# Rational layer: the order of VectorE's subtraction after ScalarE's reads of the tile h

## The chip, the cores and the metric

The kernel runs on one core of a Trainium2 chip. The metric is the device time of one execution in microseconds (us); the time of a kernel is the median of its runs. A profiled execution also has a span: the time from its first to its last instruction.

## The reference, cut to what matters

Three layers run one after the other: a recurrent attention over 4 x 8 heads and 768 steps, a mixture of 8 experts on 3072 tokens of width 320, and a rational layer on the same tokens. Only the last is touched:

```python
def _moe2_ref(x, w_in, w_out, a, b):        # x [3072, 320], w_in [320, 2048], w_out [2048, 320]
    h = x @ w_in
    h2 = h * h
    h3 = h2 * h
    P = a[0] + a[1] * h + a[2] * h2 + a[3] * h3
    Q = 1.0 + np.abs(b[0]) * np.abs(h) + np.abs(b[1]) * h2
    g = P / (Q + 1e-06)
    return g @ w_out
```

## The kernel before, in words

Matrix products are done to nearly full fp32 precision with split operands: a value v becomes a rounded high part and the rest v - high (low part), and each product is the sum of high x high, low x high and high x low.

**Tiling of the rational layer.** The 3072 tokens are cut into 8 groups of 384. In each group the 2048 columns of `w_in` are cut into 8 pieces of 256. One piece of one group is a step m; there are 64 steps, numbered m = 8 G + mm, with mm from 0 to 7. A step's two halves of 128 columns land in two PSUM banks of the tile `h`, which has three banks of 128 x 512: the middle bank always holds the second half, and the first half alternates between the outer banks, bank 2 in even and bank 0 in odd steps (`outer`, L1150). So in every step one outer bank holds no part of the step's own product.

**The steps' order** is written out by hand (list `order`, L1318, run by `s3_step`, L1324), with the lag of each piece of work in steps. For each engine, in the order of its queue in step m:
- TensorE: `g_in(m)` (L1181): 8 matmuls into the outer bank (called A here), in some steps three transposes (below, called T), 8 matmuls into the middle bank (B); then `g_out(m-4)` (L1288): 18 matmuls into the output banks (O).
- ScalarE: `e_gh(m-3)` (L1277), then in some steps the copy of the transposed columns (L1077), then `e_p1(m)` (L1211, line 1214) and `e_abs(m)` (L1222), both reading h of both halves, `e_u(m)` for m < 7 only (L1230), and `e_y(m-1)` (L1255) and `e_s(m-1)` (L1261), which write the PSUM tile `s` (one buffer from step 3 on).
- VectorE: `e_t(m-2)` (L1265), `e_r(m-2)` (L1269), in some steps `e_prep(m)` (L1199), `e_g(m-2)` (L1273), then `e_p2(m)` (L1242) and `e_p3(m)` (L1247), which read h.
- GpSimd: `e_gl(m-3)` (L1284), `e_u(m)` from m = 7 on (L1232), `e_w(m)` (L1238), and in the steps mm = 4, 5 and 6 the scatter of one finished output tile (L129).

**Preparing the next group.** The 384 x 320 inputs of the next group have to be transposed into three pieces of columns (kk = 0, 1, 2) and split. This lies in the last three steps of a group, mm = 5, 6 and 7, of the groups 0 to 6: 21 steps, called prep steps here; the others are called plain. In a prep step `g_prep` (L1170) uses the free outer bank: TensorE transposes into it (L1101), ScalarE copies it into the high part `xh` (or `xr` for kk = 2; `xsplit`, part 0, L1077), and later, where `e_prep` stands in the order, VectorE subtracts the high part from it (`xsplit`, part 1, L1082) into the low part `xl` (for kk = 2 into the upper half of `xr`).

**What waits for what.** The framework orders readers of one PSUM tile on different engines after each other, and it takes `h` as one tile, whichever bank is meant. Where the kernel wants no order it says so: `other_bank` (L1165) declares that two instructions do not depend on each other, and `bank_free` (L1158) adds the wait that is needed. `sr["reads", m]` is the list of the instructions that have read h of step m so far: when `e_prep(m)` is called it holds `e_p1(m)` and `e_abs(m)`, both of ScalarE.

Of the kernel before, what the change touches and what calls it, by code (L numbers as in the profile page):

```python
# [8 lines left out]
F32 = mybir.dt.float32  # L9
# [5 lines left out]
ALU = mybir.AluOpType  # L15
# [6 lines left out]
def kernel(  # L22
# [17 lines left out]
    nc = tc.nc  # L40
# [100 lines left out]
    sx, sr = {}, {}  # L141
# [211 lines left out]
    with actx:  # L353
# [24 lines left out]
        for _ in range(12):  # L378
# [11 lines left out]
            out=bmask, in_=bmask, compare_op=ALU.is_ge, fill=0.0, base=0,  # L390
# [3 lines left out]
            out=bmask, in_=bmask, compare_op=ALU.is_ge, fill=0.0, base=D - 1,  # L394
# [512 lines left out]
        for g in range(3):  # L907
# [4 lines left out]
            out=grpf, in0=grpf, in1=cend.unsqueeze(1).broadcast_to([NH, B * 3, NCH]), op=ALU.mult  # L912
# [125 lines left out]
        out=mall, in0=macc.unsqueeze(1).broadcast_to([128, NE, JS, NE]),  # L1038
        in1=perm.unsqueeze(2).broadcast_to([128, NE, JS, NE]), op=ALU.mult,
# [30 lines left out]
    def xsplit(kk, pt, xs, part=None):  # L1070
        n = pt.shape[1]
        if part != 1:
            if kk < 2:
                xs += [xp.tile([128, 512], F32R, name=f"x{v}{kk}", bufs=2)[:, 0:n] for v in "hl"]
            else:
                xs.append(xp.tile([128, 512], F32R, name="xr", bufs=2)[:, 0:n])
            hi = nc.scalar.activation(out=xs[2 * kk], in_=pt, func=AF.Copy)  # L1077
            if part == 0:
                return hi.ins
        if part != 0:  # L1080
            xh, xl, r = (xs[2 * kk], xs[2 * kk + 1], slice(0, 128)) if kk < 2 else (xs[4], xs[4], slice(64, 128))
            nc.vector.tensor_tensor(out=xl[r], in0=pt[r], in1=xh[r].bitcast(F32), op=ALU.subtract)  # L1082

    wouth_d = dram.tile([DFF, DM], F32, name="wouth_d")
    woutl_d = dram.tile([DFF, DM], F32, name="woutl_d")
# [79 lines left out]
    def other_bank(products, reads):  # L1165
        for p in products:
            for r in reads:
                tc.declare_no_dep(p, r, reason="another bank")

    def g_prep(G, kk, m):  # L1170

        pt = sr["h"][:, outer(m + 1), 0:TG]
        bank_free(transposes(sx["xt4", NE + G], kk, pt), m - 1)
        sr["prep", m] = (kk, pt, sx["x", NE + G])
        sr["pcopy", m] = xsplit(*sr["prep", m], part=0)
        if kk == 2:
            ids = xp.tile([128, 4], I32, name="ids", bufs=3)
            nc.gpsimd.tensor_copy(ids[:, 0:NJ], sx["xt4", NE + G][:, 0:NJ, XI - 1].bitcast(I32))
            sx["ids", NE + G] = ids
# [18 lines left out]

    def e_prep(m):  # L1199
        if ("prep", m) in sr:  # L1200
            xsplit(*sr["prep", m], part=1)

    def tl(pool, name, tag, bufs, dt=F32):
        return pool.tile([128, 2, TG], dt, name=name, tag=tag, bufs=bufs)
# [104 lines left out]
    def e_store(m, j):  # L1309
# [8 lines left out]
    order = [  # L1318
        (3, e_gh), (3, e_gl), (LAG + 1, e_osb), (0, g_in), (0, e_p1), (0, e_abs), (0, e_u), (0, e_w), (LAG, g_out),
        (2, e_t), (2, e_r), (0, e_prep), (2, e_g), (1, e_y), (1, e_s), (0, e_p2), (0, e_p3),  # L1320
        *((LAG + 1 + j, e_store, j) for j in range(NJ)),
    ]
# [10 lines left out]
    with ExitStack() as mctx:  # L1333
# [95 lines left out]
        def x_prep(e, kk, pt=None):  # L1429
            n = width(e) if e < NE else TG  # L1430
            if pt is None:
                pt = ps_t.tile([128, 512], F32, name="pt")[:, 0:n]
            transposes(sx["xt4", e], kk, pt)
            xsplit(kk, pt, sx["x", e])
            if kk == 2:
                j = (n + 127) // 128
                if e < NE:
                    g0 = e * JS + slots(e)[0]
                    nc.gpsimd.tensor_copy(head[:, g0:g0 + j, :], sx["xt4", e][:, 0:j, 0:XI])
                else:  # L1440
                    ids = xp.tile([128, 4], I32, name="ids", bufs=3)
                    nc.gpsimd.tensor_copy(ids[:, 0:j], sx["xt4", e][:, 0:j, XI - 1].bitcast(I32))
                    sx["ids", e] = ids
# [99 lines left out]
        with tc.tile_pool(name="ov", bufs=1) as ov, tc.tile_pool(name="ovp", bufs=1, space=PSUM) as ovp:  # L1543
            total = nc.values_load(cnt_i[:, NE:NE + 1], min_val=0, max_val=NT)
            with tc.If(total > 0):
# [20 lines left out]
                for e in range(NE):  # L1566
                    n_e = nc.values_load(nt_i[:, e:e + 1], min_val=0, max_val=NTILE)
                    with tc.If(n_e > 0):
# [3 lines left out]
                            out=mk, in0=ekey, scalar1=float(NE - e), scalar2=-(2.0**20), op0=ALU.is_equal, op1=ALU.mult  # L1572
# [6 lines left out]
                        for t in range(NTILE):  # L1579
                            nc.gpsimd.indirect_dma_start(  # L1580
                                out=over[:, :], out_offset=bass.IndirectOffsetOnAxis(ap=idx[:, t:t + 1], axis=0),
# [5 lines left out]
                            out=mk, in0=tokf, scalar1=past[:, e:e + 1], scalar2=2.0**20, op0=ALU.is_ge, op1=ALU.mult  # L1587
# [6 lines left out]
                        with tc.For_i(0, n_e, 1) as t:  # L1594
# [3 lines left out]
                                out=xo, out_offset=None, in_=x_rows[:, :],  # L1598
# [21 lines left out]
                            for _ in gates(ov, go, xo[:, 0:XI].unsqueeze(1), "o"):  # L1620
# [3 lines left out]
                                out=yo[:, 1:], in0=py, scalar1=go, scalar2=None, op0=ALU.mult  # L1624
                            )
                            nc.gpsimd.indirect_dma_start(
                                out=y_sorted[:, :], out_offset=bass.IndirectOffsetOnAxis(ap=ix[:, 1:2], axis=0),
# [20 lines left out]
        for n in range(NB + LAG2):  # L1648
# [30 lines left out]
            if n == 2:  # L1679
# [5 lines left out]
                    out=t4, in0=t4, scalar=2.0**20, in1=slot, op0=ALU.mult, op1=ALU.add  # L1685
# [149 lines left out]
```

## Time and profile before

| what | value |
|---|---|
| median of 3 runs | 876.54 us (875.67 to 881.92) |
| the profiled execution's own time | 871.06 us |
| its span | 869.3 us |
| the 64 steps of the rational layer lie from about | 446 us to the end of the span |
| the last of the 21 prep steps ends before | 804.43 us |
| TensorE matmul busy over the span | 769.0 us (88%) |
| VectorE busy | 746.9 us (86%) |
| GpSimd busy | 591.5 us (68%) |
| ScalarE busy | 489.7 us (56%) |

Times of instructions are microseconds from the start of the span unless marked ns. PE is TensorE's matmul, PEld its weight load, DVE VectorE, ACT ScalarE, POOL GpSimd. "[1.79 <-ACT A L1222]" behind an instruction says that its engine stood idle for 1.79 us before it and that the instruction of line 1222 on ScalarE, which writes A, ended the wait. In rows of busy time by stretch the columns are the stretch, its length, the busy time (and instructions) of PE, PEld, DVE, ACT and POOL, the granted clock of TensorE as a share of its full speed, the busy share of the DMA engines and GB/s. Rows of the chain give start, length and what it was. Matmuls overlap in the pipeline: what one of them costs is read from one start to the next.

### The profile page before, as it was taken

What the parts mean: (1) busy time and instruction counts of PE and PEld (TensorE: products, weight loads), DVE (VectorE), ACT (ScalarE), POOL (GpSimd) and SP (SyncE); (2) the same over time, 40 slices, a digit from 0 to 9 for tenths busy, and PEclk for the clock granted to TensorE, in tenths of its full rate; (3) what the DMA queues carried; (4) which work ended last, traced back from release to release, by engine and by line L of the source; (5) the groups of instructions that cost most, each with busy time, mean ns of one, the idle gap of its engine ahead of it and who ended that gap; (6) DMA issues with size and microseconds to landing.
All of it is one profiled execution on the core that took longest, in us unless ns stands there. A gap on an engine that the chain in (4) does not pass through costs nothing.

```text
span 869.3 us, 14447 instructions
## 1 busy us (share of the span) xinstructions
PE 769.0 (88%) x4724; PEld 710.7 (82%) x4724; DVE 746.9 (86%) x1421; ACT 489.7 (56%) x839; POOL 591.5 (68%) x595
## 2 busy tenths in 40 slices
PE   9988889878788988888898899898989899898994
PEld 5777777777777878778897899897989899897984
DVE  8999999997599999999888787887878788787882
ACT  5343434233445544344548777676767767676772
POOL 7645353565377685678854688787887878787882
PEclk7999999999899999999999999999999999999997
DMA  8988788435376564775863030101010010000000
GB/s 208 277 251 233 229 238 225 145 110 151 103 209 190 169 196 146 229 225 179 254 214 122 15 108 16 31 8 39 1 46 1 16 31 16 8 9 16 1 24 24
DMA packets 86965, 102.43 MB, mean 118 GB/s; under 512 B 7915, under 2 KB 79219, under 8 KB 86880
## 3 DMA queue, kind: packets, MB, share of 16 engines
q1 hardware_dynamic: 82976, 88.63, 35.5%
q0 software_dynamic: 3904, 12.77, 4.4%
q8 instruction: 40, 0.66, 0.3%
q14 instruction: 45, 0.37, 0.1%
HBM read 84.01 MB, written 17.93 MB: 117 GB/s over the span
## 4 chain that ended last, share of the span: by engine, by line
PE 33%; DVE 20%; ACT 6%; issue 5%; DMA 4%; POOL 3%; SPq 2%; POOLq 0%; DVEq 0%; ACTq 0%
PE h L228 17%; PE yb L1298 4%; PE yb L1300 4%; PE yb L1299 4%; DVE P L1247 3%; ACT P L1214 3%; DVE P L1242 2%; DVE P L1273 2%; PE ph L228 2%; ACT A L1222 2%; DVE hl L1455 2%; DMA raw<-in_w_in 1%; DMA r<-in_w 1%; DVE vt L1380 1%; DVE xl L1082 1%
## 5 line engine op out<-in xcount | busy, mean ns | idle before, releaser
L1238 POOL TENSOR_TENSOR U<-U,A 128x768 f32<-128x768 f32 (+1 forms) x65 | 118.7, 1826 | 30.3 <-ACT U L1230 25.6
L1284 POOL TENSOR_TENSOR gl<-P,gh 128x768 fp32r<-128x768 f32 x63 | 117.7, 1869 | 11.5 <-ACT gh L1281 10.8
L1300 PE MATMUL yb<-wo,gl 128*128 128x320 f32 x384 | 120.2, 313 | 1.7 <-POOL gl L1284 1.7
L1298 PE MATMUL yb<-wo,gh 128*128 128x320 f32 x384 | 120.1, 313 | 1.2 <-ACT gh L1281 1.2
L1299 PE MATMUL yb<-wo,gh 128*128 128x320 f32 x384 | 119.9, 312 | 0.0
L1214 ACT ACTIVATE P<-h,coef 128x768 f32<-128x768 f32 (+1 forms) x65 | 63.9, 983 | 71.9 <-PE h L228 71.9
L192 POOL TENSOR_TENSOR l<-r,h 128x384 fp32r<-128x384 f32 x64 | 66.2, 1057 | 54.3 <-ACT h L183 54.1
L228 PE MATMUL h<-xh,winh 128*128 128x384 f32 x256 | 91.0, 356 | 12.9 <-DVE P L1247 12.8
L228 PE MATMUL h<-xh,winl 128*128 128x384 f32 x256 | 86.3, 337 | 0.0
L228 PE MATMUL h<-xl,winh 128*128 128x384 f32 x256 | 86.3, 337 | 0.0
L1232 POOL TENSOR_SCALAR U<-A,coef 128x768 f32<-128x768 f32 x56 | 55.1, 983 | 42.0 <-ACT A L1222 42.0
L1242 DVE TENSOR_TENSOR P<-P,h 128x768 f32<-128x768 f32 (+1 forms) x65 | 61.1, 940 | 24.7 <-ACT A L1222 20.3
L1469 PE MATMUL yb<-h,hh 128*128 128x320 f32 (+1 forms) x216 | 68.7, 318 | 9.9 <-DVE ysb L1483 6.3
L1255 ACT ACTIVATE s<-U,coef 128x768 f32<-128x768 f32 (+1 forms) x62 | 55.4, 894 | 35.3 <-DVE P L1273 35.2
L1300 PEld LDWEIGHTS yb<-wo,gl 128*128 128x128 f32 x384 | 73.3, 191 | 2.2 <-POOL gl L1284 2.2
L1298 PEld LDWEIGHTS yb<-wo,gh 128*128 128x128 f32 x384 | 73.3, 191 | 1.5 <-ACT gh L1281 1.5
L228 PE MATMUL ph<-xh,h 128*128 128x256 f32 (+4 forms) x152 | 56.3, 370 | 19.4 <-DVE hl L1455 14.4
L1299 PEld LDWEIGHTS yb<-wo,gh 128*128 128x128 f32 x384 | 73.3, 191 | 0.0
L1471 PE MATMUL yb<-h,hl 128*128 128x320 f32 (+1 forms) x216 | 67.9, 314 | 0.0
L1470 PE MATMUL yb<-l,hh 128*128 128x320 f32 (+1 forms) x216 | 67.9, 314 | 0.0
L1247 DVE SCALAR_TENSOR_TENSOR P<-P,coef,h 128x768 f32<-128x768 f32 (+1 forms) x65 | 65.2, 1003 | 2.3
L1273 DVE SCALAR_TENSOR_TENSOR P<-P,coef,s 128x768 f32<-128x768 f32 (+1 forms) x62 | 62.0, 1000 | 1.7
(693 smaller groups left out, 2374.0 us busy)
## 6 DMA issues: line engine op xcount, KB each, us to landing
fb<-fz_d SPq DMA_DIRECT2D x22, 512.0 KB
r<-in_w SPq DMA_DIRECT2D x32, 320.0 KB
r<-in_w SPq DMA_DIRECT2D x32, 256.0 KB
raw<-in_w_out SPq DMA_DIRECT2D x16, 320.0 KB
r<-in_w SPq DMA_DIRECT2D x64, 64.0 KB
raw<-in_w_in SPq DMA_DIRECT2D x32, 128.0 KB
x_rows<-xt SPq DMA_DIRECT2D x24, 164.5 KB
xt<-y_sorted SPq DMA_DIRECT2D x8, 481.5 KB
```

The costliest lines, as they stand in the source:

```text
L228: mms = [nc.tensor.matmul(ps, lhsT=a, rhs=b, start=(i == 0), stop=(i == 7)) for i, (a, b) in enumerate(seq)]
L1214: r = nc.scalar.activation(out=part("P", m, i), in_=part("ph", m, i), func=AF.Identity, scale=coef[:, 3:4], bias=coef[:, 2:3])
L1238: eng.tensor_tensor(out=U, in0=U, in1=part("A", m, i), op=ALU.mult)
L1242: r = nc.vector.tensor_tensor(out=P, in0=P, in1=part("ph", m, i), op=ALU.mult)
L1247: r = nc.vector.scalar_tensor_tensor(out=P, in0=P, scalar=coef[:, 1:2], in1=part("ph", m, i), op0=ALU.add, op1=ALU.mult)
L1273: nc.vector.scalar_tensor_tensor(out=P, in0=P, scalar=coef[:, 0:1], in1=part("S", m, i), op0=ALU.add, op1=ALU.mult)
L1284: eng.tensor_tensor(out=part("gl", m, i), in0=part("P", m, i), in1=part("gh", m, i).bitcast(F32), op=ALU.subtract)
L1298: nc.tensor.matmul(y, lhsT=gh[:, i, t], rhs=wh, start=first, stop=False)
L1299: nc.tensor.matmul(y, lhsT=gh[:, i, t], rhs=wl, start=False, stop=False)
L1300: nc.tensor.matmul(y, lhsT=gl[:, i, t], rhs=wh, start=False, stop=last)
L1469: nc.tensor.matmul(y, lhsT=hh[:, js], rhs=h2[:, half, :], start=(fb == 0), stop=False)
L1470: nc.tensor.matmul(y, lhsT=hh[:, js], rhs=l2[:, half, :], start=False, stop=False)
```

## The change

`xsplit` hands back the subtraction that it issues, and `e_prep` declares that this subtraction does not depend on the reads of h that the step has listed so far (`e_p1` and `e_abs` of the same step, in the two other banks). The order of the instructions on each engine stays as it is.

```diff
@@ xsplit
         if part != 0:
             xh, xl, r = (xs[2 * kk], xs[2 * kk + 1], slice(0, 128)) if kk < 2 else (xs[4], xs[4], slice(64, 128))
-            nc.vector.tensor_tensor(out=xl[r], in0=pt[r], in1=xh[r].bitcast(F32), op=ALU.subtract)
+            return nc.vector.tensor_tensor(out=xl[r], in0=pt[r], in1=xh[r].bitcast(F32), op=ALU.subtract).ins
@@ e_prep
     def e_prep(m):
         if ("prep", m) in sr:
-            xsplit(*sr["prep", m], part=1)
+            other_bank([xsplit(*sr["prep", m], part=1)], sr["reads", m])
```

## Rows read from the trace of the kernel before

**Rows 1.** Busy time by stretch: one of seven, their sum, plain steps, one step.
```profile
531.35:558.52 27.17, 23.47 (x147) 22.44 (x146) 20.72 (x24) 18.15 (x25) 21.91 (x17) 1.00 0.12 37
...
sum 190.28, PE 164.35 PEld 157.15 DVE 144.53 ACT 128.84 POOL 150.03; mean PE 23.48 PEld 22.45 DVE 20.65 ACT 18.41 POOL 21.43
...
558.52:580.52 22.00, 22.00 (x138) 21.59 (x137) 19.24 (x21) 17.11 (x24) 18.63 (x13) 1.00 0.00 1
...
538.60:545.80 7.20, 5.99 (x37) 5.67 (x37) 5.28 (x8) 4.66 (x7) 5.93 (x5) 1.00 0.08 25
```

**Rows 2.** Waits from 476 to 808 us: who for whom, total, times, longest.
```profile
DVE xl L1082 <- ACT A L1222: 26.6, 14, 2.5
PE h L1101 <- DVE P L1247: 16.9, 14, 1.3
DVE xr L1082 <- ACT A L1222: 13.0, 7, 1.9
```

**Rows 3.** The chain that ended last, through one prep step (mm = 6).
```profile
539.71 0.55 PE h L1101 x3
540.26 1.41 PE h L228 x8
541.69 0.99 ACT P L1214
542.68 0.71 ACT A L1222
543.42 0.56 DVE xl L1082
543.98 0.92 DVE P L1273
544.90 0.88 DVE P L1242
545.80 1.02 DVE P L1247
546.96 0.52 PE h L1101 x3
```

**Rows 4.** VectorE in order of time, the same prep step.
```profile
540.67 0.96 DVE L1269 SCALAR_TENSOR_TENSOR s<-U,s 128x768 f32<-128x768 f32 x1
543.42 0.56 DVE L1082 TENSOR_TENSOR xl<-h,xh 128x384 fp32r<-128x384 f32 x1 [1.79 <-ACT A L1222]
543.89 1.00 DVE L1273 SCALAR_TENSOR_TENSOR P<-P,coef,s 128x768 f32<-128x768 f32 x1
```

**Rows 5.** ScalarE in order of time, the same prep step.
```profile
540.29 0.49 ACT L1077 ACTIVATE xh<-h 128x384 fp32r<-128x384 f32 x1
```

**Rows 6.** TensorE in order of time: a prep step with transposes unstalled.
```profile
531.19 0.34 PE L228 MATMUL h<-xh,winh 128*128 128x384 f32 x1
...
532.60 0.49 PE L1101 MATMUL h<-ident,xt 128*128 128x128 f32 x3
...
536.97 0.34 PE L228 MATMUL h<-xh,winh 128*128 128x384 f32 x1
```

**Rows 7.** VectorE in order of time: a plain step, a third prep step.
```profile
528.88 1.02 DVE L1273 SCALAR_TENSOR_TENSOR P<-P,coef,s 128x768 f32<-128x768 f32 x1
...
531.47 1.01 DVE L1247 SCALAR_TENSOR_TENSOR P<-P,coef,h 128x768 f32<-128x768 f32 x1
...
550.64 0.56 DVE L1082 TENSOR_TENSOR xr<-h,xr 64x384 fp32r<-64x384 f32 x1 [1.85 <-ACT A L1222]
551.23 1.01 DVE L1273 SCALAR_TENSOR_TENSOR P<-P,coef,s 128x768 f32<-128x768 f32 x1
```

**Rows 8.** ScalarE in order of time, the same plain step.
```profile
528.75 0.99 ACT L1214 ACTIVATE P<-h,coef 128x768 f32<-128x768 f32 x1 [0.46 <-PE h L228]
```

**Rows 9.** Busy time by stretch, around TensorE's longest wait in this layer.
```profile
473.00:476.30 3.30, 0.01 (x1) 0.01 (x1) 3.27 (x4) 3.27 (x4) 2.48 (x2) 1.00 0.00 0
...
478.00:480.00 2.00, 2.00 (x9) 2.00 (x8) 1.97 (x2) 1.84 (x3) 0.80 (x1) 0.50 0.00 0
```

## The prediction

> **What bounds the kernel now.** The change touches only the 21 prep steps, so I read the busy time by stretch first, cut so that each stretch runs from the start of a group's first prep step over four steps (mm = 5, 6, 7 and the next group's mm = 0). One of them takes 27.17 us and all seven 190.28 us, so 27.18 us each in the mean, with TensorE busy for 23.48 us [rows 1]. Four plain steps take 22.00 us, with TensorE busy all the time [rows 1]. So plain steps are bound by TensorE, at 5.50 us each, and prep steps are not: 3.70 us of each of those stretches TensorE stands idle, at full granted clock.
>
> The waits say for what. TensorE's transposes waited 14 times for VectorE's `e_p3`, 16.9 us in all, and VectorE's subtraction waited 21 times, once in each prep step, for ScalarE's `e_abs`: 26.6 + 13.0 = 39.6 us, some 1.9 us each [rows 2]. The chain that ended last joins the two [rows 3]: transposes 0.55, B 1.41, `e_p1` 0.99, `e_abs` 0.71, subtraction 0.56, `e_g` 0.92, `e_p2` 0.88, `e_p3` 1.02, and then the next transposes. From 539.71 to 546.96 that is 7.25 us with the small gaps. It is a closed loop: the next step's T and B need the banks that `e_p3` reads last, so its length is the length of a prep step. TensorE alone would need less: a prep step whose transposes did not stall ran from 531.19 to 536.97, which is 5.78 us [rows 6].
>
> Two pieces of that loop have no business in it. The subtraction needs the copy `xh` alone, which ended at 540.29 + 0.49 = 540.78 [rows 5], while VectorE was free when `e_r` ended at 540.67 + 0.96 = 541.63; it started at 543.42 after 1.79 us of idleness [rows 4]. And `e_g`, which belongs to a step two earlier, stands behind it in VectorE's queue.
>
> **The change, part by part.** No instruction is added, removed or put elsewhere on its engine, and no DMA is touched. One wait goes: that of the subtraction for `e_p1` and `e_abs`.
>
> *What moves.* The subtraction can start when both the copy and `e_r` have ended, at 541.63 in the step shown, ends by 542.19, and `e_g` by 543.11 (0.56 + 0.92 from the chain). `e_abs` hands over at about 543.40. Both then lie wholly beside ScalarE's reads, with 0.29 us to spare.
>
> *What is late next.* `e_p2` still waits for `e_abs`; it does so in plain steps too. The loop loses 0.56 + 0.92 = 1.48 us: 7.25 - 1.48 = 5.77 us. Built from a plain step it comes out alike: from the start of T to `e_p1` 541.69 - 539.71 = 1.98 us [rows 3], and from `e_p1` at 528.75 [rows 8] to the end of `e_p3` at 531.47 + 1.01 = 532.48 [rows 7] 3.73 us, together 5.71. The 1.98 has a stalled start of T in it. TensorE itself is ready after 5.78 us [rows 6], so it becomes the bound again, by less than 0.1 us. Margins so thin hold elsewhere: `e_p3` of that plain step ends 0.12 us before T at 532.60 [rows 6], and TensorE does not stall.
>
> *Sum.* Four steps become 3 x 5.78 + 5.50 = 22.84 us, seven stretches 159.88 us, against 190.28 us now: 30.4 us less. Counted the other way: 3.70 us idle in a stretch, and some 0.2 us more at each of three stalls because the pipeline drains and refills, gives 4.3 us, times 7 = 30.1 us. From the profiled execution's own 871.06 us this gives 840.7 us (its span was 869.3 us). The median of the runs stands 5.48 us above that execution, so the forecast is 876.54 - 30.4 = 846.1 us, rounded to 846.
>
> *Costs at nothing, and their cover.* The subtraction and `e_g` now run beside `e_p1` and `e_abs`, all four reading PSUM. The trace has a near case: in a plain step `e_g`, which reads the PSUM tile `s`, runs from 528.88 beside `e_p1` from 528.75, and they take 1.02 and 0.99 us [rows 7, 8], no more than `e_p1` takes with VectorE idle (0.99, [rows 3]). That is 0 per step. No row shows the subtraction itself beside a read of `h`; the far bound is that VectorE's and ScalarE's reads take turns, which puts the 1.48 us back and gives 0 gain. I take 0, the value of the nearest row, and keep the other end as a rival.
>
> VectorE's cover of 0.29 us is thinner where instructions hand over more slowly: `e_g` starts 543.89 - 543.42 = 0.47 us after an `xl` subtraction [rows 4] and 551.23 - 550.64 = 0.59 us after an `xr` one [rows 7], which works on the upper 64 partitions only. If the handover from `e_r` to the `xr` subtraction cost as much, 0.1 to 0.2 us of the cover would go, nothing of the time. Uncovered it would be 7 x 0.2 = 1.4 us.
>
> By the Trainium skill, "VectorE: DVE Perf Modes", section "Two Vector instructions with no wait between them", an instruction whose operands start in another quarter of the partitions than those of the one before is held until all earlier VectorE work has finished. By that rule the 64-partition subtraction, which so far was held by ScalarE anyway, would be held behind `e_r`, and `e_g` behind it again; rows 7 show the second of these (0.59 us, against 0.47 in rows 4), and no run shows the first. By the rule the sum stays as it is while VectorE has cover, and loses at most the 1.4 us without it.
>
> GpSimd is busy for 5.93 us in a prep step with a scatter [rows 1], which is more than 5.78. In a stretch it has 21.91 us of work [rows 1] for 22.84 us, so it falls behind by some tenths and catches up; its results are used a step later, so I cost this at nothing. ScalarE has 18.15 us and VectorE 20.72 us of work in a stretch [rows 1].
>
> **The rivals.**
>
> *GpSimd or a handover becomes the bound.* If prep steps come to 6.0 us (GpSimd's 5.93 and issue gaps) instead of 5.78, 21 x 0.22 = 4.6 us of the gain go: 851 us. For it: 96% busy. Against: the work waits a step before it is needed.
>
> *Another wait takes about half.* Prep steps of 6.5 us would cost 21 x 0.72 = 15 us: 861 us. I see no instruction in the queues that would do it: after `e_g` VectorE has only `e_p2`, and ScalarE's `e_y`, which by the code waits for `e_g` (the tile `s` has one buffer), becomes free earlier.
>
> *The wait stays.* The subtraction may be ordered behind ScalarE by something else than the two reads named, or readers of PSUM may take turns: 876.5 us. Against: the declared pair is just the one that the trace names (`e_abs`, 21 of 21 times [rows 2]), and rows 7 and 8.
>
> *Slower: TensorE's clock.* The prep stages become as dense as the plain ones. If the granted clock fell to the lower level there, each us of TensorE's work would cost a second one. The prep steps hold 21 x 5.78 = 121 us of it; from 30.4 us on, a quarter, the kernel would be slower than before, and if all of it ran so it would take 846 + 121 = 967 us. For it: the clock does fall in this layer, to 0.50 (1.2 of 2.4 GHz) at 478 us [rows 9]. Against: it fell after TensorE had done nothing from 473.0 to 476.3 us [rows 9], not after dense work, and through 22 us of dense plain steps it is 1.00 [rows 1].
>
> **How the numbers follow.** The forecast has 0.84, GpSimd or a handover 0.07, half 0.04, the wait that stays 0.03, slower 0.02. The first two hold over 8 in 10: below 846 I allow 5 us, the distance between the profiled execution and the median; above, the first rival's 851 and some 4 us for the spread of the runs (875.67 to 881.92). The range is 841 to 855 us. A measurement of this kernel tells about 1% from no change. Faster by over 1% are the first three cases, 0.95; within 1% the wait that stays, 0.03; slower 0.02.
>
> **What would show it.** Right: TensorE's transposes no longer wait for `e_p3`, stretches of four steps take 22.8 to 23.1 us with TensorE busy throughout, the subtraction starts right behind `e_r` and no longer names `e_abs`, `e_p2` takes its place as the one that waits for `e_abs`, by 0.3 to 0.5 us, and the chain runs through TensorE's A, B and O in prep steps as it does in plain ones. ScalarE's `e_y` no longer waits for `e_g`. Wrong: idle time in front of the transposes, or `e_p1` longer than 0.99 us beside the subtraction, or the subtraction still waiting for ScalarE's `e_abs`, or a granted clock below 1.00 in those stretches.

## The result and the profile after

The changed kernel takes 844.77 us in the median of 4 runs (840.93 to 845.91), the kernel before 876.11 us in its 4 runs. The ratio is 0.9623, with a 95% interval of 0.9569 to 0.9677. The forecast was 846 us, between 841 and 855.

First the busy time by stretch of the changed kernel, cut as in [rows 1]: the first and the second group's four steps from the first prep step on, the sum of all seven, four plain steps and one prep step. The columns are those of [rows 1].

```profile
487.84:511.16 23.32, 23.23 (x147) 22.49 (x146) 20.14 (x23) 19.86 (x27) 18.81 (x14) 1.00 0.05 16
533.16:556.07 22.91, 22.91 (x147) 22.44 (x146) 20.73 (x24) 18.12 (x25) 21.91 (x17) 1.00 0.14 44
...
sum 160.74, PE 160.65 PEld 157.18 DVE 144.49 ACT 128.53 POOL 150.37; mean PE 22.95 PEld 22.45 DVE 20.64 ACT 18.36 POOL 21.48
...
556.07:578.05 21.98, 21.98 (x137) 21.59 (x137) 19.23 (x21) 17.12 (x24) 18.65 (x13) 1.00 0.00 1
538.95:544.74 5.79, 5.79 (x38) 5.69 (x38) 5.28 (x7) 4.59 (x7) 5.52 (x5) 1.00 0.09 31
```

Where TensorE stood idle for 3.70 us of every 27.17 [rows 1] it now never stops from the second group on, and a prep step takes 5.79 us. The seven stretches went from 190.28 to 160.74 us: 29.5 us. Plain steps are what they were.

The chain that ended last, through the second group's prep steps, answers to [rows 3]:

```profile
533.16 1.41 PE h L228 x8
534.90 1.41 PE h L228 x8
538.95 1.41 PE h L228 x8
540.69 1.41 PE h L228 x8
544.74 1.41 PE h L228 x8
```

No ScalarE and no VectorE is left in it: A, B, A, B (with O and T between them, not shown), all TensorE's. And the waits of the layer (440 to 790 us, with all 21 prep steps in it), to be laid beside [rows 2]:

```profile
DVE P L1242 <- ACT A L1222: 20.7, 41, 1.8
POOL U L1232 <- ACT A L1222: 18.6, 25, 0.8
DVE xl L1082 <- PE h L228: 3.6, 13, 0.4
DVE xr L1082 <- PE h L228: 1.9, 6, 0.3
```

The 39.6 us in front of the subtraction have become 5.5 us, and another engine ends them: TensorE, with a matmul into h. The transposes' wait for `e_p3` (16.9 us before) is gone from the list. VectorE and ScalarE in order of time through one prep step (mm = 6) and VectorE through the next one show it closely, as [rows 4, 5, 7] did:

```profile
540.98 0.96 DVE L1269 SCALAR_TENSOR_TENSOR s<-U,s 128x768 f32<-128x768 f32 x1
542.20 0.56 DVE L1082 TENSOR_TENSOR xl<-h,xh 128x384 fp32r<-128x384 f32 x1 [0.27 <-PE h L228]
542.68 1.01 DVE L1273 SCALAR_TENSOR_TENSOR P<-P,coef,s 128x768 f32<-128x768 f32 x1
543.86 0.95 DVE L1242 TENSOR_TENSOR P<-P,h 128x768 f32<-128x768 f32 x1 [0.18 <-ACT A L1222]
...
548.03 0.56 DVE L1082 TENSOR_TENSOR xr<-h,xr 64x384 fp32r<-64x384 f32 x1 [0.31 <-PE h L228]
548.63 1.01 DVE L1273 SCALAR_TENSOR_TENSOR P<-P,coef,s 128x768 f32<-128x768 f32 x1
549.70 0.95 DVE L1242 TENSOR_TENSOR P<-P,h 128x768 f32<-128x768 f32 x1
```

```profile
542.14 1.00 ACT L1214 ACTIVATE P<-h,coef 128x768 f32<-128x768 f32 x1 [0.92 <-PE h L228]
543.03 0.80 ACT L1222 ACTIVATE A<-h 128x768 f32<-128x768 f32 x1
```

The subtraction starts with `e_p1`, 0.06 us behind it, and not behind `e_r`. Subtraction, `e_g`, `e_p1` and `e_abs` run side by side and take 0.56, 1.01, 1.00 and 0.80 us. Before, one after the other, they took 0.56 and 1.00 [rows 4], 0.99 [rows 3] and, in ScalarE's order of time of the kernel before:

```profile
542.59 0.80 ACT L1222 ACTIVATE A<-h 128x768 f32<-128x768 f32 x1
```

The two profiled executions lie only 25.15 us apart (871.06 and 845.91). The one of the changed kernel came to its first prep step at 487.84 us, the one before at 482.15, 5.69 us later, through work that the change does not touch; from there to the end of the span it took 356.36 us against 387.15. Such differences lie within the spread of the runs, so the stretches are compared here, not the spans.

### The profile page after: what moved, and what is told of

It is laid out like the page before. It is cut to its first block, busy times and chain, and to the rows that moved or that the text cites. A ratio compares the mean times of both kernels' runs of the same rounds, so it can differ in the third digit from the quotient of the medians.

```text
span 844.2 us, 14447 instructions
## 1 busy us (share of the span) xinstructions
PE 769.7 (91%) x4724; PEld 712.9 (84%) x4724; DVE 749.7 (89%) x1421; ACT 488.6 (58%) x839; POOL 595.4 (71%) x595
## 4 chain that ended last, share of the span: by engine, by line
PE 47%; DVE 12%; DMA 4%; issue 3%; ACT 3%; POOL 2%; SPq 1%; POOLq 0%; ACTq 0%; DVEq 0%
PE h L228 20%; PE yb L1300 6%; PE yb L1298 6%; PE yb L1299 6%; PE ph L228 4%; DMA r<-in_w 2%; DVE hl L1455 2%; DMA raw<-in_w_out 2%; DVE head L1058 1%; DVE nrmg L1784 1%; PE yb L1469 1%; PE yb L1470 1%; PE yb L1471 1%; PE h L1101 1%; DVE ct L1375 1%
## 5 line engine op out<-in xcount | busy, mean ns | idle before, releaser
L228 PE MATMUL ph<-xh,h 128*128 128x256 f32 (+4 forms) x152 | 56.2, 370 | 21.2 <-DVE hl L1455 16.9
L1265 DVE SCALAR_TENSOR_TENSOR U<-U,s 128x768 f32<-128x768 f32 (+1 forms) x62 | 58.0, 935 | 4.4 <-ACT s L1261 4.3
```

Of the source, the lines that this page charges most:

```text
L228: mms = [nc.tensor.matmul(ps, lhsT=a, rhs=b, start=(i == 0), stop=(i == 7)) for i, (a, b) in enumerate(seq)]
```

## The experiments

The theory: a prep step was a closed loop through `e_p3`, with the subtraction and `e_g` in it; taking both out puts TensorE at the bound. Its rivals: that the wait alone was the price; that gains are given back a step later; that the place of the subtraction is what counts; that TensorE now has room to spare; that VectorE's loop still sets the pace. Lines of VectorE's instructions move down by one to three in some of the kernels. Each ratio is to the kernel before, run beside it (a median of 875.72 us for the first four kernels, 875.04 us for the others). Several of the differences are hardly larger than the spread of the runs, so what is read is the stretch of four steps and the rows beside it.

**The wait kept, `e_g` put ahead of it** (on the kernel before):

```diff
-        (2, e_t), (2, e_r), (0, e_prep), (2, e_g), (1, e_y), ...
+        (2, e_t), (2, e_r), (2, e_g), (0, e_prep), (1, e_y), ...
```

> The kernel before, with the wait kept, but e_g put ahead of the subtraction in VectorE's order. If a prep step is the closed loop of the prediction, only e_g's 0.92 us leaves it: prep steps of about 6.3 us, a stretch of four steps from 27.18 to 24.4 us, and 21 x 0.92 = 19 us off the time: about 857 us against 876. The rival, that the wait for ScalarE's two reads is what costs and e_g only stands there by chance, gives no gain or nearly none: a stretch of 26.5 to 27.2 us and 870 to 876 us.

Measured: 856.02 us, ratio 0.9797 (0.9718 to 0.9876). A stretch of four steps, and VectorE's subtraction:

```profile
531.31:555.73 24.42, 23.49 (x146) 22.44 (x146) 20.72 (x24) 17.86 (x25) 21.89 (x17) 1.00 0.13 42
```
```profile
536.22 0.56 DVE L1082 TENSOR_TENSOR xl<-h,xh 128x384 fp32r<-128x384 f32 x1 [0.88 <-ACT A L1222]
```

The subtraction still waits for `e_abs`, and two thirds of the gain are there. So the larger term is `e_g`'s 0.92 us, a piece of work that does not depend on what was waited for and only stood behind it in the queue. The rival's 26.5 to 27.2 us are out.

**The change for the second prep step alone:**

```diff
-            other_bank([xsplit(*sr["prep", m], part=1)], sr["reads", m])
+            low = xsplit(*sr["prep", m], part=1)
+            if sr["prep", m][0] == 1:
+                other_bank([low], sr["reads", m])
```

> The change for the second of the three prep steps alone (kk = 1). If each step's loss stands by itself, a stretch falls by 1.4 us to 25.8 us and the time by 7 x 1.4 = 10 us to about 866. The rival, that a gain in one prep step is given back as a longer wait in the next, leaves the stretch at 27.2 us and the time at 876; if the steps help each other, it falls by more than 1.5 us.

Measured: 864.06 us, ratio 0.9881 (0.9814 to 0.9949). The stretch, and VectorE's three subtractions in it:

```profile
530.75:556.56 25.81, 23.36 (x147) 22.45 (x146) 20.74 (x24) 18.14 (x25) 21.93 (x17) 1.00 0.12 39
```
```profile
535.67 0.56 DVE L1082 TENSOR_TENSOR xl<-h,xh 128x384 fp32r<-128x384 f32 x1 [1.93 <-ACT A L1224]
...
541.18 0.56 DVE L1082 TENSOR_TENSOR xl<-h,xh 128x384 fp32r<-128x384 f32 x1
...
548.67 0.56 DVE L1082 TENSOR_TENSOR xr<-h,xr 64x384 fp32r<-64x384 f32 x1 [1.97 <-ACT A L1224]
```

27.18 - 25.81 = 1.37 us, a third of the whole 4.27. The neighbours wait about as before (1.93 and 1.97 us, in the kernel before 1.92 and 1.85): nothing is given back.

**The subtraction put last**, behind `e_p3`, without the change:

```diff
-        (2, e_t), (2, e_r), (0, e_prep), (2, e_g), (1, e_y), (1, e_s), (0, e_p2), (0, e_p3),
+        (2, e_t), (2, e_r), (2, e_g), (1, e_y), (1, e_s), (0, e_p2), (0, e_p3), (0, e_prep),
```

> The kernel before with the subtraction put behind e_p3, at the end of VectorE's part of the step, where ScalarE's reads are long over. If only the loop through e_p3 counted, this would be as good as the change: stretches of 22.9 us, 845 us. My theory says that the subtraction is then late for something else: the next step's A writes the bank that it reads, so A waits for it and the loop becomes A 1.41, T to e_p1 1.98, e_p1 to e_p3 3.73, subtraction 0.55: about 7.7 us for each step that follows a prep step, a stretch of 28.5 us, slower than before by 7 x 1.3 = 9 us: about 885 us.

Measured: 887.26 us, ratio 1.0134 (1.0067 to 1.0201), slower than before. Two of its stretches, a wait of TensorE in the second of them and the time behind it, and then TensorE in order of time:

```profile
534.69:563.42 28.73, 23.57 (x147) 22.64 (x146) 20.81 (x24) 17.88 (x25) 21.83 (x17) 1.00 0.10 35
585.42:615.68 30.26, 25.10 (x146) 24.17 (x146) 20.81 (x24) 17.86 (x25) 21.77 (x17) 0.94 0.10 33
606.50:608.40 1.90, 0.11 (x1) 0.00 (x0) 1.82 (x4) 1.54 (x3) 1.82 (x2) 1.00 0.26 94
608.46:612.50 4.04, 4.04 (x14) 4.04 (x15) 2.81 (x3) 0.00 (x0) 2.01 (x2) 0.58 0.00 0
```
```profile
600.57 0.44 PE L228 MATMUL h<-xh,winh 128*128 128x384 f32 x1 [1.66 <-DVE xl L1082]
```

The subtraction waits for nothing there, and the kernel loses: A of the next step writes the bank that the subtraction reads, and waits for it 1.7 to 1.9 us (the three waits of the second stretch). The stretch of 28.73 is the 28.5 of the theory. What it did not say is the second one, 30.26.

**VectorE's cover, measured by more work**: the change, and the subtraction three times over in the first two prep steps (the same values are written again).

```diff
-            other_bank([xsplit(*sr["prep", m], part=1)], sr["reads", m])
+            for _ in range(3 if sr["prep", m][0] < 2 else 1):
+                other_bank([xsplit(*sr["prep", m], part=1)], sr["reads", m])
```

> The change with the subtraction issued three times over in the first two prep steps (the same values twice more): VectorE gets 2 x 0.47 = 0.94 us more in 14 steps. If the loop through VectorE now lies just under TensorE's time, with the 0.18 us of idleness before e_p2 as its only cover, a prep step grows by 0.76 us, a stretch from 22.90 to 24.4 us, the time by 10.6 us to about 855. With the 0.29 us of cover of the prediction it would be 24.2 us. The rival, that TensorE alone sets the pace with room to spare, leaves 22.9 us and 845 us.

Measured: 858.12 us, ratio 0.9806 (0.9744 to 0.9869). The stretch, VectorE in the first prep step, and its three copies one by one, from the chain that ended last:

```profile
531.37:556.10 24.73, 23.25 (x146) 22.45 (x146) 22.96 (x28) 18.16 (x25) 21.92 (x17) 1.00 0.12 41
```
```profile
534.62 1.74 DVE L1082 TENSOR_TENSOR xl<-h,xh 128x384 fp32r<-128x384 f32 x3 [0.26 <-PE h L228]
536.28 1.00 DVE L1274 SCALAR_TENSOR_TENSOR P<-P,coef,s 128x768 f32<-128x768 f32 x1
537.21 0.95 DVE L1243 TENSOR_TENSOR P<-P,h 128x768 f32<-128x768 f32 x1
```
```profile
534.62 0.57 DVE xl L1082
535.22 0.57 DVE xl L1082
535.81 0.56 DVE xl L1082
```

A step grew by (24.73 - 22.90) / 2 = 0.91 us and not by the 0.76 expected. The expectation had the added work too small: it took 0.47 us for a copy, the time from a subtraction to the `e_g` behind it, but here each copy starts only when the one before has ended, so the third starts 535.81 - 534.62 = 1.19 us after the first. Of these 1.19 us 0.28 do not show. That is VectorE's cover, and the rows give nearly the same: from `e_g` to `e_p2` it is 543.86 - 542.68 = 1.18 us in the changed kernel and 537.21 - 536.28 = 0.93 us here, where `e_p2` waits for nothing, so 0.25 us are slack. The idle time of 0.18 us understates it, because one instruction on VectorE starts before the last has ended. Beyond this cover added work costs time: that TensorE sets the pace with room to spare is out.

**The changed kernel once more:**

> The changed kernel once more, to stand beside the next ones on the same chip: 842 to 848 us, stretches of 22.90 us.

Measured: 848.06 us, ratio 0.9694 (0.9646 to 0.9743), with runs from 843.09 to 852.80: just above what was expected, with the stretches as they were (22.92 us). The interval overlaps the first one's.

**The subtraction free of B as well**, so that it needs only the copy `xh`:

```diff
@@ g_in
             products = mm3(ph[:, i, :], winh, winl, slice(f0, f0 + 128), sx["x", NE + G])
...
+            if n == 1:
+                sr["second", m] = products
@@ e_prep
-            other_bank([xsplit(*sr["prep", m], part=1)], sr["reads", m])
+            other_bank([xsplit(*sr["prep", m], part=1)], sr["reads", m] + sr["second", m])
```

> The change, and the subtraction declared free of the step's 8 matmuls into the middle bank (B), for whose end it now waits 0.26 to 0.31 us in the trace. If TensorE is the bound, the subtraction starts right behind e_r, e_p2's idle time grows from 0.18 to about 0.45 us, and the stretch stays at 22.90 us and the time within 2 us of the changed kernel. The rival, that VectorE's part of the loop still sets the pace of prep steps, gives a stretch shorter by 0.3 us or more.

Measured: 844.03 us, ratio 0.9635 (0.9594 to 0.9677). The stretch, and VectorE in order of time (first the third prep step of the first group, then the first one of the second):

```profile
529.62:552.52 22.90, 22.90 (x147) 22.46 (x146) 20.54 (x24) 17.88 (x25) 21.91 (x17) 1.00 0.13 44
```
```profile
498.75 0.96 DVE L1271 SCALAR_TENSOR_TENSOR s<-U,s 128x768 f32<-128x768 f32 x1
499.74 0.56 DVE L1082 TENSOR_TENSOR xr<-h,xr 64x384 fp32r<-64x384 f32 x1
...
531.66 0.96 DVE L1271 SCALAR_TENSOR_TENSOR s<-U,s 128x768 f32<-128x768 f32 x1
532.53 0.55 DVE L1082 TENSOR_TENSOR xl<-h,xh 128x384 fp32r<-128x384 f32 x1
533.00 1.00 DVE L1275 SCALAR_TENSOR_TENSOR P<-P,coef,s 128x768 f32<-128x768 f32 x1
534.54 0.95 DVE L1244 TENSOR_TENSOR P<-P,h 128x768 f32<-128x768 f32 x1 [0.54 <-ACT A L1224]
```

The idle time before the subtraction is gone, that before `e_p2` grew from 0.18 to 0.54 us, and the stretch is the same. That shows what the wait of 0.27 us was, the end of B, and that TensorE is the bound. The time lies 0.7 us below the changed kernel's first median and 4.0 us below the one beside it, where at most 2 us were expected; the intervals overlap.

**Free of B, and three times over:**

> The same, with the subtraction issued three times over in the first two prep steps. The cover is then 0.18 + 0.27 = 0.45 us, so that 0.94 - 0.45 = 0.49 us show in each of 14 steps: a stretch of 23.9 us and about 852 us, between the changed kernel and the same tripling with the wait for B (24.4 us). If the wait for B takes no cover away, it comes out as that one, 24.4 us.

Measured: 854.32 us, ratio 0.9746 (0.9701 to 0.9790). Its stretch, and VectorE's subtractions with what follows them:

```profile
533.58:557.71 24.13, 23.26 (x146) 22.45 (x146) 22.76 (x28) 18.09 (x25) 21.91 (x17) 1.00 0.13 43
```
```profile
536.48 1.73 DVE L1082 TENSOR_TENSOR xl<-h,xh 128x384 fp32r<-128x384 f32 x3
538.13 1.00 DVE L1276 SCALAR_TENSOR_TENSOR P<-P,coef,s 128x768 f32<-128x768 f32 x1
539.05 0.95 DVE L1245 TENSOR_TENSOR P<-P,h 128x768 f32<-128x768 f32 x1
```

A step grew by (24.13 - 22.90) / 2 = 0.61 us, 0.30 less than with the wait for B, and more than the 0.49 expected, for the reason given at the first tripling. The work added is the same, 538.13 - 536.48 - 0.47 = 1.18 us, so the cover is 0.57 us here. The order behind B thus took 0.30 us out of the cover, unseen as long as there was some.

**The tile s in PSUM one step earlier**, on the kernel free of B. This goes for TensorE's wait at the head of the layer, of which [rows 9] show the counterpart:

```diff
-    MS = 3
+    MS = 2
```

> The kernel free of B, with the PSUM tile s used from step 2 on instead of step 3 (MS = 2). e_t, e_r and e_g of step 2 then read s in PSUM; in the trace e_r of that step took 2.47 us with its operand in SBUF beside GpSimd's work and 0.96 us later. If that 1.5 us lies in TensorE's wait of 3.8 us at the head of the layer, that wait and the stretch at the lower clock behind it shrink and the kernel comes out 1 to 4 us below the one free of B; if the wait hangs on e_g of step 1 alone, nothing changes.

Measured: 848.16 us, ratio 0.9691 (0.9636 to 0.9745), no faster than the kernel free of B. VectorE at the head of the layer:

```profile
475.67 2.46 DVE L1275 SCALAR_TENSOR_TENSOR P<-P,coef,S 128x768 f32<-128x768 f32 x1
...
480.94 0.96 DVE L1271 SCALAR_TENSOR_TENSOR s<-U,s 128x768 f32<-128x768 f32 x1
...
484.78 0.95 DVE L1244 TENSOR_TENSOR P<-P,h 128x768 f32<-128x768 f32 x1 [1.82 <-ACT A L1224]
```

`e_r` of step 2 fell from 2.47 us (in the kernel free of B) to 0.96 us as meant, and VectorE then waited 1.82 us for `e_abs`. TensorE's wait stayed, 3.80 us there and 3.82 us here: the time was not on the path. `e_g` of step 1 stands at 2.46 us, but no run took that away, so that it makes TensorE's wait is argued, not shown. No kernel here is shown to be faster than the changed one.

## Why the prediction was right

*The loop.* The prediction took 1.48 us out of a loop of 7.25 and let TensorE's 5.78 us decide. Prep steps take 5.79. The larger of the two terms stands by itself: with only `e_g` out (the swap) a stretch fell by 2.76 us, 0.92 per step and exactly that term. The subtraction's 0.56 has no such run: with it out as well a stretch fell by another 24.42 - 22.91 = 1.51 us, 0.50 per step, and went no lower, because TensorE took over.

*The sum.* 22.84 us for a stretch were 22.90 in six groups and 23.32 in the first. The first group's rest is a term that the prediction did not have. For m < 7 `e_u` is ScalarE's, which is busy for 19.86 us in this stretch against 18.12 in the next, and in the shorter steps its queue is late, so that VectorE's `e_t` waits for `e_s`:

```profile
495.51 0.96 DVE L1265 SCALAR_TENSOR_TENSOR U<-U,s 128x768 f32<-128x768 f32 x1 [0.75 <-ACT s L1261]
```

It made 0.4 us in all; the cause is read from the trace, and no run moved it. The some 0.2 us for each stall, of the prediction's second count, are borne out: TensorE's busy time in the seven stretches fell from 164.35 to 160.65 us, 0.18 us for each of 21 stalls. Together 29.5 us of 30.4 came; the medians lie 876.11 - 844.77 = 31.3 us apart, and the ratio's interval, 28 to 38 us, holds both.

*Where it was wrong.* "The subtraction can start when both the copy and `e_r` have ended" failed: the two reads of ScalarE had hidden another order behind them, that of B's writes to the same tile, and it came to light when they went. So two of its signs did not come: the subtraction starts behind B and not right behind `e_r`, and `e_p2` waits 0.18 us for `e_abs`, or not at all in the third prep step, and not 0.3 to 0.5 us. That the cover still measures 0.28 us where the prediction had 0.29 is luck, for two errors cancel. B's order took 0.30 us from it. Against that, the cover without that order is larger than the 0.29 us. The prediction put VectorE's pieces end to end, 0.96 + 0.56 + 0.92 = 2.44 us from the start of `e_r` to the earliest start of `e_p2`, but they overlap: the kernel free of B gives 0.87 + 0.47 us to `e_g`, and the tripling on it 0.92 us from there, 2.26 us together. And `e_abs` lets `e_p2` start 534.54 - 531.66 = 2.88 us after `e_r` there, not 543.40 - 540.67 = 2.73 us. In the third prep step the cover is thinner still, 549.70 - 548.63 = 1.07 us from `e_g` to `e_p2`, 0.14 us more than the 0.93 where nothing waits. The forecast held because a cover that is just long enough costs as little as a long one; 0.3 us more of VectorE's work per step would have shown, as the tripling did.

*The rivals.* GpSimd's waits for `e_abs` fell from 39.0 to 18.6 us, and it delayed nobody that the list of waits shows. It falls behind in the prep steps and catches up in the plain one, as forecast: its `e_u` starts 6.02, 5.96, 6.10 and 4.82 us apart in the second group's four steps. Reads of PSUM did not take turns: the four durations stayed, `e_p1` at a median of 0.992 us before and 0.995 after. The granted clock is 1.00 in all seven stretches. `e_y`, which waited 32.5 us for `e_g` before, waits for it no longer, as forecast, but for 0.4 us in the first group.

*The 64-partition subtraction.* In the kernel free of B it starts 499.74 - 498.75 = 0.99 us after `e_r` started, when `e_r` has ended, and the full one 532.53 - 531.66 = 0.87 us after. That fits the hold that the Trainium skill states in "VectorE: DVE Perf Modes", section "Two Vector instructions with no wait between them"; the trace agrees, with 0.12 us, which cost nothing here.

## What to carry to other kernels

An instruction that waits also holds up what is queued behind it on its engine; when the wait lies on a closed loop of engines, price the work behind it as well (here 0.92 us against 0.56), and moving that work ahead of the wait is a cure by itself. Taking an order between readers away can uncover one with a writer, so list every order that the framework sets on the instruction, not only the one that the trace names. And before an instruction is moved behind the wait instead, look who needs the buffer that it holds: the subtraction put last cost 1.3%.

## What the hardware showed

With the subtraction put last TensorE waits 1.7 to 1.9 us three times in a row. In the stretch from 585.42 us the granted clock then fell: it was 1.00 through the third wait (606.50 to 608.40, 0.11 us of work) and 0.58 in the mean of the next 4.04 us, most of which ran at 0.50, the lower of the two levels (1.2 of 2.4 GHz). The stretch took 30.26 us instead of 28.73, so the fall cost 1.5 us beside the waits. One more of the seven stretches, from 739.12 us, is the same: 30.27 us, with a mean clock of 0.94. In the other five, as in that from 534.69 us with the same waits, the stretch is 28.73 us and the clock stayed at 1.00, as it did with the waits of 1.2 us of the kernel before [rows 1, 2]. Short waits of TensorE can thus cost more than they last, and not each time; what set the two stretches apart is not shown.
